# Attention and FFN in one kernel: engines in written order, value copies on ScalarE, later attention dealt out over the FFN halves

## Chip, cores and metric

One core of a Trainium2 chip. The metric is device time in microseconds (us) of one execution; the kernel before takes 285.56 us (median of three, 284.75 to 286.89). In this text PE is TensorE, PEld its weight loads, DVE is VectorE, ACT is ScalarE and POOL is GpSimd.

## The reference, cut to what matters

```python
# q, k, v: (4, 8, 768, 64); sort_net: (4, 8, 8, 8); x for the FFN: 3072 tokens x 512
P = sort_net
for _ in range(5):                       # Sinkhorn: exp, rows, columns
    P = exp(P - max(P)); P = P / P.sum(-1); P = P / P.sum(-2)
k_sorted = einsum('bhij,bhjcd->bhicd', P, k_blocks)     # 8 blocks of 96 tokens
v_sorted = einsum('bhij,bhjcd->bhicd', P, v_blocks)
attn = softmax(q_block @ k_sorted_block.T / 8)          # inside each block
x = (attn @ v_sorted_block) -> (3072, 512)
out = (silu(x @ w_gate) * (x @ w_val)) @ w_out          # d_ff = 1536
```

## The kernel before

The work falls into batches (4), each batch into two halves of 384 tokens. The K/Q step mixes blocks on PE and drains PSUM to SBUF. For V, the block index and head sit on the partitions and `(c, d)` on the free axis, so a copy first turns `(c, d)` into `(d, c)` (tile `vch`). A "unit" is QK, exp, AV, normalise, transpose for four blocks of two heads; four units give one half its input. The FFN of one half is called an FFN half below; there are eight.

```python
for it in range(N_ITER):                          # Sinkhorn, small tiles
    nc.scalar.activation(p_sb, p_sb, AF.Exp)
    nc.vector.reduce_sum(rowred[:, :, 0], p_sb, axis=AX.X)
    ...                                           # reciprocal, mul, and the same by columns

def drain(dst, src):                              # PSUM drains: DVE and ACT in turn
    if tog[0] % 2 == 0: nc.vector.tensor_copy(dst, src)
    else:               nc.scalar.copy(dst, src)
    tog[0] += 1

def emit_vch(pair):                               # pair 0 on DVE, pair 1 on GpSimd
    nat = v_tiles[pair]
    for s in range(4):
        cs = slice(s * (C // 4), (s + 1) * (C // 4))
        eng = nc.gpsimd if pair else nc.vector
        eng.tensor_copy(vch[:, :, cs], nat[:, cs, :].transpose([0, 2, 1]))
...
emit_att(0)
for b in range(B):                                # a scheduler orders the engines by priority
    if b + 1 < B: emit_att(b + 1)
    emit_gv(b, 0); emit_gv(b, 1)                  # gate and value products of both halves
    emit_out(b, 0); emit_out(b, 1)                # output products
```

The softmax here doesn't subtract the row's maximum and nothing guards it: scores larger than these inputs give would overflow.

## Time and profile before

| | before |
|---|---|
| median | 285.56 us |
| PE busy | 90% |
| first matmul, first complete FFN input, last matmul | 13.6, about 46, 281.3 us |

The page of the profile of the kernel before: busy time per engine, then rows of 40 equal slices of the span (about 7.1 us each), a digit being the busy share in tenths; PEclk is the granted PE clock.

```profile
span 285.9 us, 6221 instructions
...
PE 257.2 (90%) x2600; PEld 152.7 (53%) x2608; DVE 178.9 (63%) x383; ACT 121.7 (43%) x246; POOL 39.1 (14%) x51
...
PE   0077799969999999999999999999999999999993
...
ACT  2036745437633215976534215764332134343211
...
PEclk9999955979999999999999999999999999999999
```

PE is at 9 tenths from the sixth slice on, but for the ninth (57 to 64 us) and the last. Most of what is lost is lost before about 66 us. The chain of work that ended last, kernel before (start us, length us, what), shows how:

```profile
16.65 1.51 DVE vch L204
...
19.35 1.19 DVE vch L204
...
21.97 1.40 DVE vch L204
...
46.31 1.28 PE v_ps L297 x4
...
50.22 0.65 PE g_ps L288 x4
```

DVE copies values between the drains of K/Q, on the chain. At 46.31 us four matmuls of 384 columns take 1.28 us; at 50.22 us they take 0.65 us. That is the half clock and the full one, read from durations.

### The profile page before, as it was taken

Reading aid. Unit: us, or ns where it says so; the run is one execution under the profiler, and the core shown is the slowest. Engines: PE = TensorE matmul, PEld = TensorE weight load, DVE = VectorE, ACT = ScalarE, POOL = GpSimd, SP = SyncE. Lnnn points to the kernel's source line nnn. Section 1 sums busy time; section 2 is a strip of 40 time slices with the busy share of each in tenths; the row PEclk is TensorE's granted clock in tenths of the full one; section 3 lists DMA queues with packets and bytes.
Section 4 is the critical chain, followed back from the end, with each engine's and each line's share of the span. In section 5 each row is a group of like instructions: output and inputs, shape, how many; then the busy total and the mean of one; then the engine's idle time right before and its main releaser. Section 6 shows DMA issues by size and latency. Waiting matters only on the chain.

```text
span 285.9 us, 6221 instructions
## 1 busy us (share of the span) xinstructions
PE 257.2 (90%) x2600; PEld 152.7 (53%) x2608; DVE 178.9 (63%) x383; ACT 121.7 (43%) x246; POOL 39.1 (14%) x51
## 2 busy tenths in 40 slices
PE   0077799969999999999999999999999999999993
PEld 0066555746655446666655446666555445555441
DVE  6798746937988205789988304699885018888300
ACT  2036745437633215976534215764332134343211
POOL 8557421029500000000000000000000000000000
PEclk9999955979999999999999999999999999999999
DMA  6999999999100122000000122000000220000021
GB/s 99 198 203 197 200 213 204 220 214 214 38 0 1 39 110 76 2 2 0 3 0 2 38 110 76 2 2 2 0 0 2 111 102 10 0 0 3 37 110 73
DMA packets 13659, 20.84 MB, mean 73 GB/s; under 512 B 1088, under 2 KB 8768, under 8 KB 13632
## 3 DMA queue, kind: packets, MB, share of 16 engines
q0 software_dynamic: 10128, 14.16, 28.2%
q1 hardware_dynamic: 3504, 6.30, 5.8%
q8 instruction: 20, 0.33, 0.4%
q14 instruction: 7, 0.06, 0.1%
HBM read 28.32 MB, written 6.29 MB: 121 GB/s over the span
## 4 chain that ended last, share of the span: by engine, by line
PE 82%; DVE 11%; ACT 3%; issue 2%; ACTq 0%
PE v_ps L297 22%; PE g_ps L288 22%; PE o_ps L308 22%; PE av_ps L245 4%; PE qk L230 4%; PE tkq L193 3%; PE x_ps L255 3%; PE tv L214 3%; DVE kqt L180 2%; DVE vch L204 1%; DVE st L251 1%; ACT vt L182 1%; DVE vt L180 1%; ACT th_sb L291 1%; DVE colred L136 0%
## 5 line engine op out<-in xcount | busy, mean ns | idle before, releaser
L288 PE MATMUL g_ps<-xt,wg_sb 128*128 128x384 bf16 x384 | 84.8, 331 | 0.2 <-DVE h L299 0.2
L297 PE MATMUL v_ps<-xt,wv_sb 128*128 128x384 bf16 x384 | 82.1, 331 | 0.0
L291 ACT ACTIVATE th_sb<-g_ps 128x384 bf16<-128x384 f32 x96 | 47.1, 491 | 63.2 <-PE g_ps L288 62.6
L293 DVE SCALAR_TENSOR_TENSOR gs_sb<-th_sb,g_ps 128x384 bf16<-128x384 bf16 x96 | 52.9, 551 | 26.9 <-ACT th_sb L291 20.9
L308 PE MATMUL o_ps<-wo_sb,h 128*128 128x512 bf16 x280 | 62.4, 379 | 0.4
L299 DVE SCALAR_TENSOR_TENSOR h<-v_ps,gs_sb 128x384 bf16<-128x384 f32 x96 | 53.1, 553 | 9.0 <-PE v_ps L297 0.8
L297 PEld LDWEIGHTS <-wv_sb 128*128 128x128 bf16 x384 | 36.8, 98 | 24.5 <-issue 0.8
L288 PEld LDWEIGHTS <-wg_sb 128*128 128x128 bf16 x384 | 36.2, 99 | 23.5 <-issue 2.3
L308 PEld LDWEIGHTS <-h 128*128 128x128 bf16 x288 | 28.2, 98 | 33.6
L180 DVE CAST kqt<-tkq 128x512 bf16<-128x512 f32 x24 | 15.9, 688 | 33.9 <-PE tkq L193 33.9
L311 ACT COPY o_sb<-o_ps 128x512 f32<-128x512 f32 x24 | 14.1, 586 | 51.4 <-PE o_ps L308 51.4
L235 ACT ACTIVATE er<-qk 96x384 bf16<-96x384 f32 x64 | 27.1, 487 | 12.2 <-PE qk L230 12.2
L193 PE MATMUL tkq<-rmix,kq 128*64 128x64 bf16 x768 | 20.3, 212 | 5.5 <-issue 2.5
L193 PEld LDWEIGHTS <-kq 128*64 128x64 bf16 x768 | 17.7, 126 | 8.9 <-issue 7.9
L251 DVE TENSOR_TENSOR st<-av_ps,r_sb 96x512 bf16<-96x512 f32 x32 | 21.9, 684 | 0.8
L182 ACT CAST kqt<-tkq 128x512 bf16<-128x512 f32 x24 | 14.1, 586 | 15.7 <-PE tkq L193 15.6
L230 PE MATMUL qk<-kqt 64*128 64x96 bf16 x256 | 14.0, 217 | 1.9 <-DVE kqt L180 1.4
L245 PE MATMUL av_ps<-vt,er 96*128 96x65 bf16 x256 | 14.9, 202 | 0.2 <-ACT vt L182 0.2
L180 DVE CAST vt<-tv 96x512 bf16<-96x512 f32 x16 | 12.2, 785 | 2.7 <-PE tv L214 2.5
L182 ACT CAST vt<-tv 96x512 bf16<-96x512 f32 x16 | 12.5, 787 | 2.1 <-PE tv L214 1.8
L214 PE MATMUL tv<-vmix,vch 128*128 128x128 bf16 x128 | 12.4, 236 | 1.0 <-DVE vt L180 0.3
L255 PEld LDWEIGHTS <-st 96*128 96x128 bf16 x128 | 7.6, 101 | 10.5 <-DVE st L251 9.1
(43 smaller groups left out, 123.0 us busy)
## 6 DMA issues: line engine op xcount, KB each, us to landing
out_dram<-o_sb SPq DMA_DIRECT2D x24, 256.0 KB, 2.0
v<-in_v_dram POOLq DMA_DIRECT2D x8, 384.0 KB, 13.1
kq<-in_k_dram POOLq DMA_DIRECT2D x6, 384.0 KB, 11.6
kq<-in_q_dram POOLq DMA_DIRECT2D x6, 384.0 KB, 12.1
wg_sb<-in_moe_w_gate_dram POOLq DMA_DIRECT2D x6, 256.0 KB, 11.8
wv_sb<-in_moe_w_val_dram POOLq DMA_DIRECT2D x6, 256.0 KB, 11.1
wo_sb<-in_moe_w_out_dram POOLq DMA_DIRECT2D x1, 1536.0 KB, 18.9
kq<-in_k_dram POOLq DMA_DIRECT2D x4, 192.0 KB, 5.6
```

Of the source, the lines that this page charges most:

```text
L180: nc.vector.tensor_copy(dst, src)
L182: nc.scalar.copy(dst, src)
L193: nc.tensor.matmul(tp[two * D:(two + 1) * D, lc, :], lhsT=nat[:, cb * 8 + lc, :], rhs=rm[:, two, :], start=True, stop=True)
L230: nc.tensor.matmul(pss[two][:, i4, :], lhsT=flat[lo:lo + D, at:at + 128], rhs=kqt[lo:lo + D, 1, g, i, :], start=True, stop=True)
L235: nc.scalar.activation(e[:, 0:4 * C], pss[two][0:C].rearrange("p a c -> p (a c)"), AF.Exp, scale=scale)
L245: nc.tensor.matmul(av[:, two, i4, :], lhsT=es[two][:, i4 * C:i4 * C + 128], rhs=vt[:, 2 * g + two, half * 4 + i4, :], start=True, stop=True)
L288: nc.tensor.matmul(g_ps, lhsT=wg_sb[:, kc, ts(m, 128)], rhs=xt[:, kc, :], start=(kc == 0), stop=(kc == NKC - 1))
L291: nc.scalar.activation(th_sb, g_ps, AF.Tanh, scale=0.5)
L293: nc.vector.scalar_tensor_tensor(gs_sb, th_sb, 1.0, g_ps, op0=ALU.add, op1=ALU.mult)
L297: nc.tensor.matmul(v_ps, lhsT=wv_sb[:, kc, ts(m, 128)], rhs=xt[:, kc, :], start=(kc == 0), stop=(kc == NKC - 1))
L299: nc.vector.scalar_tensor_tensor(h_w[:, m, :], v_ps, 0.5, gs_sb, op0=ALU.mult, op1=ALU.mult)
L308: nc.tensor.matmul(o_ps, lhsT=h_w[:, m, ts(t3, 128)], rhs=wo_sb[:, m, :], start=(m == 0), stop=(m == NFC - 1))
```

## The change

The intent: fix the order of all engines until the first FFN step, take the value copies off DVE's critical place, start the FFN after four units, and deal the later attention out over the FFN halves so that PE has no attention-only stage.

```diff
+    man = tc.manual_schedule(engines={ET.PE, ET.Pool, ET.DVE, ET.Activation})
+    load_v(0, ...); load_q(0, ...); load_k(0, ...)       # then weights, then batch 1
     for it in range(N_ITER):
         nc.scalar.activation(p_sb, p_sb, AF.Exp)
+        if it >= 2:
+            copy_v(nc.scalar, 0, lowr, it - 2)           # 64 x 1536, (c d) -> (d c), on ACT
         ...
+    copy_v(nc.scalar, 0, lowr, 3)
...
+    for db in range(8):  v_chunk(0, db, "sv"[db % 2], tags[db % 2])   # batch 0 only
+    for cb in range(12): kq_chunk(0, cb, "sv"[cb % 2], tags[cb % 2])
+    for u in range(4):   ...                              # four units, then the FFN
+    man = tc.manual_schedule(engines={ET.PE, ET.Pool})    # from here only PE and POOL fixed
+    def copies(pair, rows, count):
+        return [(0.0, lambda s=s: copy_v(nc.scalar, pair, rows, s, count)) for s in range(count)]
+    merge(ffn(0), units(0, range(4, 8)) + mingle(kqs(1), copies(0, highr, 8)))
+    merge(ffn(1), [... v_chunk(1, db, "s", "att") ...] + units(1, range(4)))
+    merge(ffn(2), mingle(units(1, range(4, 8)) + kqs(2), copies(1, slice(0, 128), 8)))
+    ...                                                   # and so on to ffn(7)
-    emit_att(0)
-    for b in range(B): ...
```

In the FFN part all drains of K/Q and V are on ACT ("s"). `merge` weights pieces by an expected PE time and deals the second list out among the first.

## The prediction

> # Prediction
>
> **What bounds the kernel now.** TensorE. The page has PE 90% busy, and the chain of waits is 82% PE. Priced with dense stretches of the trace (one gate/value step 1.33 us, one output tile 2.55 us, one 8-row K/Q chunk about 0.35 us, a QK/AV/transpose unit about 0.74 us, value mixing 7 to 8 us in all), the program holds about 237 us of PE work at full clock. The last matmul ends at 281.3 us, so some 44 us are lost: 13.6 us before the first matmul (Sinkhorn), about 13 us from there to 36 us, about 12 us from 36 to 66 us, and only 6 to 7 us in the whole rest.
>
> The early losses, by the timeline: DVE does four value copies of 1.5 us between the K/Q drains (16.6 to 25.4 us); 16 value drains of 0.79 us make PE wait until 33.7 us; then units follow at 2.5 us each in a chain transpose, QK, AV, reciprocal, normalise (0.7 us). The first FFN input is complete only at about 46 us. The clock row shows half clock from about 36 to 49 us and again at 60 to 63 us, after a 2.5 us PE gap. The Trainium skill (TensorE: Matmul & The Clock Gate, Part 1) says that the clock is released only by sustained activity; the trace agrees: 384-column matmuls are 0.32 us apart until 48.9 us, then 0.16.
>
> **What changes.** Value copies for batch 0 leave DVE for ACT, between the Sinkhorn exps (estimate 1.45 us each in gaps of 1.5 us, so nearly free). Only batch 0's half of the values (8 chunks) is mixed before attention, and the FFN starts after 4 units instead of waiting behind other work. Later attention is spread over FFN halves in fixed PE order, its drains all on ACT. No PE work goes; about 1 us is added (pair 0 mixed in two halves). Loads: values first, then Q/K of batch 0, then weights; at the 200 GB/s of the page all needed for the first FFN step are there by 30 us.
>
> **On the critical path.** Matmuls start at about 13 us as before. Value chunks until 17 to 18, K/Q chunks until 23 to 25, four units at about 1.5 us each: FFN starts at 31 to 34 us, dense. Cold clock there costs about 3 us instead of about 9. Against that, fixed order brings new stalls: two AV steps back to back share one PSUM buffer (about 1 us each, four places); ACT (0.59 us K/Q drain, 0.79 us value drain, 0.49 us tanh, copies) is about as loaded as PE in the first FFN half and in the one that mixes pair 1 (2 to 3 us each). I expect 8 to 12 us of steady loss, not 6 to 7. Sum: 237 + 1 + 13 + 10 + 3 + 9 + 4.6 (tail after the last matmul) = 278; I lean a little lower, to 276.5 us.
>
> Range 268 to 285 us. Chances: faster by over 2% 0.62, within 2% 0.34, slower 0.04.
>
> **What would show it.** Right: no DVE value copies, the first FFN matmul at 31 to 34 us, clock back to full by about 40 us; PE busy about 93%; ACT busy up from 122 to about 155 us; unchanged matmul durations. Wrong: Sinkhorn ending after 12.5 us; PE waiting for ACT drains by over 8 us in total; clock low past 45 us.
>
> **What would make it wrong.** Slower: batch 1's loads land late while PE, in fixed order, waits. Faster: clock warm already during K/Q chunks, stalls hidden by PSUM buffers.

## More of the kernel before

The groups of instructions of the kernel before, by shape (out<-in, shapes, count | busy us, mean ns of one | idle before):

```profile
L182 ACT CAST kqt<-tkq 128x512 bf16<-128x512 f32 x24 | 14.1, 586 | 15.7 <-PE tkq L193 15.6
...
L204 POOL COPY vch<-v 128x1536 bf16<-128x1536 bf16 x4 | 11.2, 2878 | 0.0
...
L204 DVE COPY vch<-v 128x1536 bf16<-128x1536 bf16 x4 | 6.0, 1490 | 0.0
```

The transposing copy is on DVE and POOL here; ACT never does it. ACT's PSUM drain of 512 elements takes 586 ns. No line shows what the copy costs on ACT.

## The result, and the profile after

The changed kernel takes 298.4 us (median of four, 297.25 to 299.41), where before took 285.91 us in the runs beside it. The ratio is 1.0437 (95% interval 1.038 to 1.0494). Ratios are the mean time of one kernel's fast runs over that of the other's of the same rounds, so not quite the ratio of the medians quoted.

The page of the profile after, the same rows:

```profile
span 295.5 us, 6302 instructions
...
PE 254.5 (86%) x2672; PEld 148.6 (50%) x2672; DVE 154.2 (52%) x351; ACT 163.1 (55%) x281; POOL 18.6 (6%) x34
...
PE   0065786769999599899989899999999999999994
...
ACT  4974347996589935455787445454543353333311
...
PEclk9998559998999999999999999999999999999998
```

ACT is at 9 tenths in five of the first 14 slices (in before only in one slice, the seventeenth), and PE is at 7 tenths or less in four of those five (the second, eighth, ninth and fourteenth). The groups after, by shape, name what ACT does there:

```profile
L111 ACT COPY vch<-v 128x768 bf16<-128x768 bf16 x8 | 12.0, 1540 | 0.0
L111 ACT COPY vch<-v 64x768 bf16<-64x768 bf16 x8 | 11.9, 1506 | 0.1
...
L111 ACT COPY vch<-v 64x1536 bf16<-64x1536 bf16 x4 | 11.0, 2776 | 0.0
```

A copy of 1536 elements takes 2.78 us, not the 1.45 of the prediction; one of 768 takes 1.5 us, where the same rate would give about 0.8. Together 34.9 us of ACT, where that rate gives about 18.6 (4 x 1.45 + 16 x 0.8). The chain that ended last, after, shows that this lies on the critical path:

```profile
6.10 2.79 ACT vch L111
9.04 2.68 ACT vch L111
11.87 5.37 ACT vch L111 x2
17.29 3.59 PE tv L232 x64
...
37.93 1.28 PE v_ps L316 x4
...
53.05 0.76 PE g_ps L307 x4
...
87.74 1.40 ACT vch L111
89.14 0.76 ACT e_all L264 x2
90.16 1.53 ACT vch L111
91.69 0.77 ACT e_all L264 x2
```

From 6.1 to 17.2 us ACT copies nearly without a break; the exps of Sinkhorn stand in its queue behind copies, and the value mixing (tv) waits for the last copy. Around 90 us the copies are between the softmax exps on the chain. These are the copies of the second pair, which the code writes into the third FFN half. ACT's order is not fixed there, and the scheduler put them early: they run from 85.8 to 102.2 us, inside the second half, which ends at 108.6.

By stage, the changed kernel (window, length, PE, PEld, DVE, ACT, POOL busy, clock, DMA share, GB/s): start, first two FFN halves, the other six with the tail.

```profile
0.00:37.40 37.40, 15.80 (x355) 13.11 (x356) 21.11 (x75) 23.25 (x29) 16.52 (x30) 0.87 1.15 189
37.40:108.60 71.20, 59.68 (x643) 33.83 (x643) 34.05 (x72) 52.82 (x78) 2.06 (x4) 0.92 0.54 109
108.60:295.50 186.90, 179.04 (x1676) 101.69 (x1674) 99.07 (x204) 87.05 (x174) 0.00 (x0) 1.00 0.09 32
```

Priced as in the prediction, the first two halves hold about 52 us of dense PE work and the rest with the tail about 180 us. So 19 us are lost in the first two halves, where the prediction's sum has 9 us of steady loss for all eight and 3 for the cold clock, and only about 6 in the 187 us after. The dealt-out attention of the later halves works; the loss is early.

### The profile page after: what moved, and what is told of

Same layout as the page of the kernel before. It is cut to its first block, busy times and chain, and to the rows that moved or that the text cites. A ratio compares the mean times of both kernels' runs of the same rounds, so it can differ in the third digit from the quotient of the medians.

```text
span 295.5 us, 6302 instructions
## 1 busy us (share of the span) xinstructions
PE 254.5 (86%) x2672; PEld 148.6 (50%) x2672; DVE 154.2 (52%) x351; ACT 163.1 (55%) x281; POOL 18.6 (6%) x34
## 4 chain that ended last, share of the span: by engine, by line
PE 76%; ACT 14%; DVE 5%; issue 3%; DMA 2%; ACTq 0%; POOLq 0%
PE o_ps L326 21%; PE g_ps L307 20%; PE v_ps L316 20%; ACT vch L111 8%; PE tkq L220 5%; PE av_ps L277 3%; PE qk L257 3%; DVE st L283 2%; PE tv L232 2%; DMA v<-in_v_dram 2%; PE x_ps L294 2%; ACT e_all L264 1%; ACT th_sb L310 1%; ACT vt L189 1%; DVE gs_sb L312 1%
## 5 line engine op out<-in xcount | busy, mean ns | idle before, releaser
L307 PE MATMUL g_ps<-xt,wg_sb 128*128 128x384 bf16 x384 | 81.0, 333 | 2.5 <-ACT o_sb L329 2.2
L326 PE MATMUL o_ps<-wo_sb,h 128*128 128x512 bf16 x288 | 65.7, 379 | 0.0
L307 PEld LDWEIGHTS <-wg_sb 128*128 128x128 bf16 x384 | 32.9, 99 | 21.4 <-issue 3.0
L264 ACT ACTIVATE e_all<-qk 96x384 bf16<-96x384 f32 x64 | 27.8, 486 | 13.3 <-PE qk L257 13.1
L111 ACT COPY vch<-v 64x768 bf16<-64x768 bf16 (+2 forms) x20 | 34.9, 1774 | 0.2
L189 ACT CAST kqt<-tkq 128x512 bf16<-128x512 f32 x42 | 23.3, 591 | 11.4 <-PE tkq L220 11.3
L189 ACT CAST vt<-tv 96x512 bf16<-96x512 f32 x28 | 19.3, 746 | 4.1 <-PE tv L232 3.3
L277 PE MATMUL av_ps<-vt,e_all 96*128 96x65 bf16 x256 | 14.5, 202 | 6.6 <-DVE st L283 6.5
L277 PEld LDWEIGHTS <-e_all 96*128 96x128 bf16 x256 | 12.1, 103 | 12.3 <-DVE st L283 4.1
L281 DVE RECIPROCAL r_sb<-av_ps 96x8 f32<-96x8 f32 x32 | 6.4, 201 | 22.5 <-PE av_ps L277 22.5
## 6 DMA issues: line engine op xcount, KB each, us to landing
wg_sb<-in_moe_w_gate_dram POOLq DMA_DIRECT2D x6, 256.0 KB, 11.9
```

Source lines behind the costliest of these rows:

```text
L111: eng.copy(dst, src)
L264: nc.scalar.activation(e[:, 0:4 * C], pss[two][0:C].rearrange("p a c -> p (a c)"), AF.Exp, scale=scale)
L277: nc.tensor.matmul(o[:, two, i4, :], lhsT=e[:, i4 * C:i4 * C + 128], rhs=vt[:, 2 * g + two, half * 4 + i4, :], start=True, stop=True)
L307: nc.tensor.matmul(g_ps, lhsT=wg_sb[:, kc, ts(m, 128)], rhs=xt[:, kc, :], start=(kc == 0), stop=(kc == NKC - 1))
L326: nc.tensor.matmul(o_ps, lhsT=h_w[:, m, ts(t3, 128)], rhs=wo_sb[:, m, :], start=(m == 0), stop=(m == NFC - 1))
```

## Experiments

Ten kernels ran, in three calls; those of one call (e1 to e4; e5 to e8; e9 and e10) shared a chip and the runs of the kernel before. e1 and the runs that build on it thus ran on different chips. Told by the ratios, the gains on e1 are 4.3 (e5), 5.2 (e6), 5.3 (e7) and 2.3 us (e8), so within 0.3 us of the differences of medians given below. Theory A: ACT, made slow by the copies, holds up both the start and the first FFN halves. Rival B: the fixed order itself (one PSUM buffer for AV, the half clock). Theory C: it is the strided access that makes the copies slow on ACT; rival D: ACT is that slow for any such copy.

| run | what | median us | ratio to before (95%) |
|---|---|---|---|
| changed kernel | | 298.40 | 1.0437 (1.038 to 1.0494) |
| e1 | FFN copies on POOL | 287.53 | 1.0055 (0.9996 to 1.0113) |
| e2 | FFN copies on DVE | 290.25 | 1.0169 (1.0107 to 1.0232) |
| e3 | copies read in order, write strided | 359.33 | 1.2581 (1.2523 to 1.2639) |
| e4 | half of the start copies on POOL | 298.21 (fast ones alone 297.61) | 1.0433 (1.0371 to 1.0495) |
| e5 | e1, start copies split finer | 282.88 | 0.9904 (0.9866 to 0.9941) |
| e6 | e1, PE kept busy until the FFN | 282.32 | 0.9874 (0.9844 to 0.9904) |
| e7 | e1, no start copies (wrong result) | 282.43 | 0.9869 (0.9825 to 0.9913) |
| e8 | e1, AV steps spread | 285.46 | 0.9973 (0.9932 to 1.0015) |
| e9 | e1, e5, e6 and e8 together | 279.07 | 0.9758 (0.9725 to 0.979) |
| e10 | changed kernel, plain copies (wrong result) | 283.34 | 0.9906 (0.986 to 0.9953) |

### e1: the FFN part's copies on POOL

```diff
-        return [(0.0, lambda s=s: copy_v(nc.scalar, pair, rows, s, count)) for s in range(count)]
+        return [(0.0, lambda s=s: copy_v(nc.gpsimd, pair, rows, s, count)) for s in range(count)]
```

Expected: 

> All else as in the changed kernel; only the 16 value copies of the FFN part (23.8 us of ACT work at about 1.5 us each in the trace, against 0.8 us that the prediction assumed) go from ACT to GpSimd. Theory A (ACT, overloaded by these copies in the first two FFN halves, holds PE up): those two halves lose about 19 us against dense work, some 4 of it to the half clock; 12 to 15 us come back, so 283 to 287 us, and ACT is no longer 100% busy anywhere between 85 and 100 us. Rival B (the fixed PE order itself, with the one PSUM buffer of AV and the half clock): at most 4 us come back, 294 us or more.

Measured: 287.53 us, 10.9 us less. PE's order did not change by one instruction. The stages of e1, for the two stages after the start:

```profile
37.90:98.70 60.80, 57.81 (x639) 33.52 (x642) 34.17 (x72) 30.61 (x62) 26.44 (x22) 1.00 0.62 127
98.70:286.00 187.30, 178.16 (x1660) 101.69 (x1674) 99.07 (x204) 87.05 (x174) 0.00 (x0) 1.00 0.09 32
```

ACT's busy time in the first two halves falls from 52.8 to 30.6 us and the stage from 71.2 to 60.8; the rest stays at 187. A copy is no shorter on POOL (1.50 and 1.52 us) than on ACT; but POOL has nothing else to do there. The gain is a little under the range expected (it was 12 to 15), but it is A's, and B's limit of 4 us is passed.

### e2: the same copies on DVE

```diff
+        return [(0.0, lambda s=s: copy_v(nc.vector, pair, rows, s, count)) for s in range(count)]
```

Expected: 

> The same 16 copies on DVE, which is 52% busy. Theory A: about as e1, 283 to 288 us; a DVE copy of 64x768 should take about 0.8 us (half of the 1.49 us that 128x1536 took on DVE before), so DVE has room. Rival B: 294 us or more. If e1 gains and e2 does not, then not ACT's load but the place of the copies matters.

Measured: 290.25 us. The copies take 0.82 us each on DVE, as expected, and most of the gain is there: it is 2.7 us smaller than with POOL. In the trace PE waits 2.0 us for DVE's gate step where e1 has none: the copies stand in DVE's queue before it. The expected range missed that by about 2 us.

### e3: read in memory order, write strided (edit condensed)

```diff
-        dst = vch3[rows, :, cs];                  src = v_tiles[pair][rows, cs, :].transpose([0, 2, 1])
+        dst = vch3[rows, :, cs].transpose([0, 2, 1]);  src = v_tiles[pair][rows, cs, :]
```

Expected: 

> All value copies stay on ACT; each reads the values in memory order and writes transposed, where the changed kernel reads with a 128-byte stride and writes runs. Theory C (the strided SBUF read of 2-byte elements is what makes ACT take 1.8 ns per element where its PSUM drains take 0.84): a 64x1536 copy falls from 2.78 to about 1.5 us, a 768 one from 1.5 to 0.8 us, FFN starts 3 to 4 us earlier, and the whole takes 279 to 285 us. Rival D (any SBUF to SBUF 16-bit copy on ACT, or the strided write, costs as much): durations and time stay as they are, 296 to 300 us.

Measured: 359.33 us. Neither outcome came; the groups of e3:

```profile
L113 ACT COPY vch<-v 128x768 bf16<-128x768 bf16 x8 | 31.8, 4124 | 0.0
L113 ACT COPY vch<-v 64x768 bf16<-64x768 bf16 x8 | 31.8, 4114 | 0.1
L113 ACT COPY vch<-v 64x1536 bf16<-64x1536 bf16 x4 | 31.1, 8054 | 0.0
```

Writing with the stride is far worse than reading with it: 8.05 us for 1536 elements against 2.78. So the access pattern matters greatly, and the strided read was the better of the two. This does not yet say what a copy without any stride costs; e10 does.

### e4: two of the four start copies on POOL

```diff
+    copy_v(nc.gpsimd, 0, lowr, 1); copy_v(nc.gpsimd, 0, lowr, 3)      # before the weight loads
-        if it >= 2:
+        if it in (2, 4):
             copy_v(nc.scalar, 0, lowr, it - 2)
```

Expected: 

> Only the start: two of the four Sinkhorn-time copies move to GpSimd (ahead of its weight loads), the others stay on ACT after the exps 3 and 5. Theory A for the start (11 us of ACT copies from 6.1 to 17.2 us set when value mixing can begin): value matmuls start at about 15 us instead of 17.3, and the FFN about 2 us earlier; 295 to 297 us in all. Against it: if weight loads, now issued after the copies, come late, PE waits for weights and the time grows over 299 us.

Measured: 298.21 us, no gain (one of the four executions, 302.33 us, was slow; the median of the others is 297.61); value matmuls began at 16.95 us instead of 17.29. The timeline of e4 (start, length, engine, line, operation) shows why:

```profile
6.19 5.74 POOL L113 COPY vch<-v 64x1536 bf16<-64x1536 bf16 x2 [1.20 <-DMA v<-in_v_dram]
...
6.64 2.68 DVE L175 TENSOR_TENSOR p_sb<-p_sb,rowred 32x64 f32<-32x64 f32 x1
...
9.87 2.14 DVE L179 TENSOR_TENSOR p_sb<-p_sb,colred 32x64 f32<-32x64 f32 x1
```

The small multiply of Sinkhorn, 0.21 us elsewhere, takes 2.68 and 2.14 us while POOL copies: the POOL copies end at 9.24 and 11.93 us, and each multiply ends 0.08 us later. The Trainium skill (GPSIMD Engine Reference, section 8, Key points) says that POOL shares its SBUF interfaces with VectorE and contends with DVE instructions that have two SBUF inputs. This multiply is such an instruction, and the trace agrees. DVE's sums and reciprocals between them keep their 0.2 us. ACT's delay of the Sinkhorn chain was traded for one on DVE. In the FFN part DVE's gate step and product read PSUM as one operand; in e1 they take 553 and 555 ns on average as in the changed kernel, so no such hold shows.

### e5: start copies in eighths, over ACT and DVE

```diff
-            copy_v(nc.scalar, 0, lowr, it - 2)            # 64 x 1536
+            copy_v(nc.scalar, 0, lowr, it - 2, 8)         # 64 x 768, fits the gap
-    copy_v(nc.scalar, 0, lowr, 3)
+    for s in (3, 4):    copy_v(nc.scalar, 0, lowr, s, 8)
+    for s in (5, 6, 7): copy_v(nc.vector, 0, lowr, s, 8)
```

Expected: 

> Against e1 (copies of the FFN part on GpSimd, 287.5 us), only the start differs: the Sinkhorn-time copies are eight pieces of 64x768 (1.48 us on ACT, which fits the 1.5 us between two exps), one after each of the exps 3 to 5, two more on ACT and three on DVE (0.8 us each) after Sinkhorn. Theory (in e1 each 2.77 us copy holds the next exp up by about 1.3 us and the last ends at 17.2 us): value mixing starts at about 15.4 us instead of 17.3, FFN 2 us earlier; 285 to 286 us. Rival (what follows is bound by loads or by the half clock): no gain, 287 us.

Measured: 282.88 us, 4.6 us less than e1, more than expected. The timeline of e5, ACT:

```profile
6.18 1.50 ACT L111 COPY vch<-v 64x768 bf16<-64x768 bf16 x1
...
7.67 0.26 ACT L163 ACTIVATE p_sb<-p_sb 32x64 f32<-32x64 f32 x1
7.83 1.47 ACT L111 COPY vch<-v 64x768 bf16<-64x768 bf16 x1
...
9.43 0.26 ACT L163 ACTIVATE p_sb<-p_sb 32x64 f32<-32x64 f32 x1
```

Now the exps come about 1.8 us apart, so the short copies fit, and value mixing starts at 14.39 instead of 17.31 us. Of the 4.6 us the trace shows 3.2 as the earlier start: the last matmul of the first gate step begins at 34.70 instead of 37.91 us. The rest was not foreseen: the clock is full again at 41.0 us in e5's trace, at 49.7 in e1's, so one gate/value step fewer runs at half clock (about 1.3 us).

### e7: no copies of batch 0 at the start (wrong result)

```diff
-            copy_v(nc.scalar, 0, lowr, it - 2)
-    copy_v(nc.scalar, 0, lowr, 3)
+            nc.tensor.matmul(tp[:, ld, :], lhsT=vch[rows, at:at + 128] if b else fake[rows], rhs=mix,
```

Expected: 

> Wrong result on purpose: e1 without any copy of batch 0's values; the value mixing of batch 0 reads a constant tile instead. It bounds what the start's copies cost. Theory: exps run 1.76 us apart, last Sinkhorn step done by 11.7 us, value mixing at 13.5 to 14 us instead of 17.3; total 283.5 to 284.5 us if the 3.4 us come through whole. If less than 1.5 us come through, K/Q loads or the clock take over.

Measured: 282.43 us; value mixing starts at 12.48 us. The start's copies cost 5.1 us in e1. e5, with a right result, gets 4.6 us, but by the start alone it gets 3.2 of 5.4: the first gate step's last matmul begins at 32.54 us here.

### e6: PE kept busy until the FFN

```diff
+    def keep_warm(n):
+        w = psum.tile([128, TW], FP32, name="warm_ps", tag="gen")
+        for _ in range(n):
+            nc.tensor.matmul(w, lhsT=ident, rhs=warm, start=True, stop=True)   # never read
```

Expected: 

> e1 with 26 idle-filling matmuls on PE (128x384, results unused): 8 before the value mixing, 4 before the first QK, 2 per unit, 6 before the FFN. Theory (half clock: in e1 the 384-column matmuls are 0.32 us apart until about 49 us, 0.16 after 53; four gate/value steps and the four units pay 4 to 6 us for it): matmuls at 0.16 us spacing from before 40 us and 282 to 285 us. Rival (the waits for DVE and ACT in the units are what counts, and the fillers only stand in the way): 287 to 289 us.

Measured: 282.32 us, 5.2 us less than e1. The chain of e1, then that of e6 (start, length, what):

```profile
46.27 1.28 PE g_ps L307 x4
...
53.47 0.65 PE g_ps L307 x4
```

```profile
36.24 0.65 PE g_ps L309 x4
36.89 0.65 PE v_ps L318 x4
```

In e1 the gate step still takes 1.28 us at 46 us; in e6 it takes 0.65 us from the first. The half clock is thus worth about 5 us in e1, where the prediction had 3. The clock comes back late in e1: the clock record is at full from 49.7 us there, and from 44.7 us in the changed kernel, so it may cost less there. In e1's profile the clock row says 1.00 throughout, against its own matmul durations; the record has no entry before 49.7 us, and here the durations are to be believed.

### e8: AV steps spread

```diff
-                todo.append((0.27, lambda u=us[n - 1]: av(b, u)))
+                todo.append((0.6, lambda u=us[n - 1]: av(b, u)))
```

Expected: 

> e1 with AV steps weighted 0.6 instead of 0.27 when side work is dealt out, so that in nearly all places a gate/value step stands between two AV steps, which share one PSUM buffer. PE waited 6.5 us in e1 for the normalisation before an AV, about 2.3 of it in the start where nothing changes. Theory: 2 to 4 us gained, 283.5 to 285.5 us. Rival (other waits appear at the same places, as two QK steps now stand together at the start of a half): within 1 us of e1.

Measured: 285.46 us, 2.1 us under e1, in the expected range, but the two intervals overlap (0.9932 to 1.0015, 0.9996 to 1.0113). PE's wait for the normalisation before an AV falls from 6.5 to 1.2 us (waits of e1, then of e8: total us, times, longest):

```profile
PE av_ps L277 <- DVE st L283: 6.5, 8, 1.4
```

```profile
PE x_ps L294 <- DVE st L283: 2.9, 3, 1.3
...
PE av_ps L277 <- DVE st L283: 1.2, 3, 0.6
```

But 2.9 us of waits for it now stand before the transposes (0.4 in e1) and 3.5 us of waits for ACT before QK (1.1 in e1). So most of the wait moved, as the rival said. The clock was also full 3.0 us earlier than in e1 (46.7 against 49.7 us). How much of the 2 us is the spreading is not shown.

### e10: plain copies (wrong result)

```diff
-        dst = vch3[rows, :, cs]
-        src = v_tiles[pair][rows, cs, :].transpose([0, 2, 1])
+        run = slice(s * (C // n) * D, (s + 1) * (C // n) * D)
+        dst = vch[rows, run]
+        src = v_tiles[pair][rows].rearrange("p c d -> p (c d)")[:, run]
```

Expected: 

> Wrong result on purpose: the changed kernel with nothing moved; every value copy on ACT copies as many elements of the same type between the same tiles, but read and written in memory order, without the transpose. Theory C: such a copy takes what the prediction assumed, 0.8 us for 768 and 1.45 us for 1536 elements (0.84 ns per element), exps are no longer held up, and the kernel takes 283 to 287 us; the wrong duration is then worth 11 to 15 of the 22 us between prediction and result, and half clock and the AV waits are the rest. Rival D: ACT needs 1.7 ns per element for any copy between SBUF tiles of 16-bit elements; the durations stay 1.5 and 2.8 us and the time 297 to 300 us.

Measured: 283.34 us. The groups of e10:

```profile
L112 ACT COPY vch<-v 128x768 bf16<-128x768 bf16 x8 | 6.6, 844 | 0.0
...
L112 ACT COPY vch<-v 64x768 bf16<-64x768 bf16 x8 | 6.4, 827 | 0.1
...
L112 ACT COPY vch<-v 64x1536 bf16<-64x1536 bf16 x4 | 5.8, 1460 | 0.1
```

These are the durations that the prediction's rate gives (0.8 and 1.45 us) nearly to the digit, on the same engine and tiles. So rival D falls: an ACT copy between SBUF tiles is not slow as such. Theory C holds in this, that the transposing access is what made it slow; that the strided side must be the read was refuted by e3. Per element, by the difference of the two lengths: (1460 - 827) / 768 = 0.82 ns plain, (2776 - 1506) / 768 = 1.65 ns with the transposing read, (8054 - 4114) / 768 = 5.1 ns with the transposing write. The chain of e10:

```profile
12.54 3.57 PE tv L233 x64
...
32.94 0.48 PE g_ps L308
```

Value mixing starts at 12.54 us, as early as with no copies at all (12.48 in e7): at the assumed duration the copies do fit the gaps and are "nearly free". The last matmul of the first gate step begins at 32.94 us, inside the predicted 31 to 34.

### e9: the fixes together

The edit is those of e1, e5, e6 and e8 together.

Expected: 

> e5, e6 and e8 together on e1 (which ran 287.5 us): start copies split over ACT and DVE, PE kept busy up to the FFN, AV steps spread, FFN copies on GpSimd. They gained 4.6, 5.2 and 2.0 us one at a time. If they are separate losses, 275 to 278 us and a ratio to the kernel before of 0.963 to 0.972, faster than both kernels. If they overlap (the clock's gain is had already by the earlier start, or the instruction stall at 22 to 25 us eats it), 279 to 282 us.

Measured: 279.07 us, ratio 0.9758 (0.9725 to 0.979): 2.4% faster than the kernel before and 6.5% faster than the changed one (279.07 / 298.4). One by one the three steps on e1 gained 4.6 + 5.2 + 2.1 = 11.9 us; together 8.5. So they overlap, as the second outcome said. The page of e9:

```profile
span 277.3 us, 6355 instructions
...
PE 249.0 (90%) x2698; PEld 146.0 (53%) x2698; DVE 155.0 (56%) x354; ACT 135.3 (49%) x266; POOL 43.1 (16%) x51
```

Part of the overlap is visible. e5 alone has already shortened the half clock, which e6 cannot win again. And a wait of PE in the K/Q chunks that the page puts down to "issue" grows from 1.6 us in e1 to 3.1 us in e9. PE gets there earlier, and the wait ends less early (22.3 us in e9, 25.3 in e6, 26.4 in the changed kernel). In all eleven traces of the new order it begins after the same 222 matmuls, whatever their mix, and even in e3, where that point comes at 44.9 us. The packed traces list the packets of each DMA queue: in all eleven PE goes on 1.4 to 1.6 us after a 16 KB packet of the queue called "instruction" has ended. The 2.5 us wait at 57.4 us in the kernel before, at whose end the clock fell to half for the second time, also ends 1.5 us after such a packet. So PE most likely waits there for its next instructions (the "instruction stall" of the expectation); no run moved the fetch to test it.

## Why the prediction was wrong, point by point

- **Where the time lay before: right.** The last six halves run in 187 us in the changed kernel and in e1, about 6 us over the priced PE work. The dealt-out attention costs nearly nothing there.
- **The step that failed: "estimate 1.45 us each in gaps of 1.5 us, so nearly free".** A 64x1536 copy took 2.78 us and overran the gaps; the 768 ones took 1.5 instead of 0.8 us. No trace had this copy on ACT; the rate is that of ACT's PSUM drains (e3's expectation puts them at 0.84 ns per element). The copy reads SBUF elements of 2 bytes 128 bytes apart. The Trainium skill (SBUF — State Buffer, "Door 1: The DMA port swizzle") has a note that warns of such access: consecutive accesses in the same 16-byte line go at full speed, and each crossing to a new line pays. It names no engine and gives no size. The runs agree that the stride costs (1.65 against 0.82 ns per element on ACT); none varied the distance, so that the 16-byte line is the reason is not shown. The prediction did not use the note.
- **What that one duration was worth: 15.1 us** of the 21.9 us between forecast and result (298.4 to 283.3 in e10). Both of its places show: the start (e7: 5.1 us of copies in e1) and the first two halves (e1: 10.9 us). They add to 16, about the 15.1, so they look nearly separate; but e7 and e1 take copies off ACT altogether, where e10 makes them short. The second place was also not the planned one: the prediction looked for an overloaded ACT in the first half and in the one that mixes pair 1 (the fourth). The copies of pair 1 are written into the third, and ACT ran them in the second.
- **FFN start at 31 to 34 us, Sinkhorn by 12.5 us: wrong, for the same reason.** Sinkhorn's last step ended at 13.9 us. The first gate step was complete only at about 37.9 us, and in e10 at 33.4. One lone matmul of that step did run at 33.84 us, between the units, so the literal sign "first FFN matmul at 31 to 34 us" came true by luck; the dense FFN that it stood for came late.
- **Cold clock "about 3 us": too small as far as shown.** Keeping PE busy gained 5.2 us on e1 (e6), whose half clock lasted until 49.7 us. In the changed kernel half clock lasted until 44.7 us, not 40.
- **AV stalls, about 4 us: right in kind,** 6.5 us of waits in the changed kernel's and e1's traces. e8 moved most of them elsewhere, and its gain of about 2 us isn't clear of noise.
- **ACT load: right in kind, wrong in size.** Foreseen 155 us, measured 163.1; the copies are 16 us over, the drains somewhat under. "2 to 3 us" of ACT-bound loss in the first half became a large share of 19 us over two halves.
- **The sign.** The chance given to slower by over 2% was 0.04. The whole forecast gain was 9 us, and one duration never seen in the trace, used 20 times on an engine planned full, was worth more.

What stays open: of the 6.8 us between e10 and the forecast, the clock (about 2 us over what was allowed, if e6's gain on e1 carries over) and ACT's remaining load in the first halves (63.2 us from 32.9 to 96.1 us in e10, against 60.8 in e1) are measured in part; 1.5 us was a lean without a reason. The rest was not separated. The moment at which the clock is full again differs between the traces (41.0 us in e5, 49.7 in e1), so a difference of 1 to 2 us between two of these runs can be the clock's alone.

## What to carry to other kernels

Before an operation is moved to another engine, look for a duration of that same access pattern on that engine; if the trace has none, the estimate is a guess and the range must hold twice its size. A copy that has to sit inside a latency chain must be cut to fit the gap, or it moves the chain itself (in e5 value mixing starts 2.9 us earlier, by halving the pieces and sharing them). When PE runs in written order, one late engine stops it, so plan the fullest side engine with slack in each stage, not on average; and where that engine's own order is left to a scheduler, look in the trace for the stage in which its work really ran.

## What the Trainium skill lacked or had wrong

- SBUF — State Buffer, "Door 1: The DMA port swizzle": no size for crossing 16-byte lines on ACT. The runs: 0.82 ns per 2-byte element in order, 1.65 ns reading with a 128-byte stride, 5.1 ns writing with a 192-byte stride. On DVE the same strided read of 768 elements took 0.82 us, on POOL 1.5 us.
- ScalarE: Activation LUTs, "What ACT_TABLE_LOAD costs": one element per cycle, 0.833 ns, for every function. That holds for the plain copy (0.82 ns in e10) and not for the transposing one; the page does not say so.
- Runtime: NRT & Kernel Launch, "Instruction fetch mechanics": says that crossing a block of 256 instructions is mostly hidden. In eleven traces PE stood for 1.2 to 3.3 us after the same 222 matmuls and went on 1.4 to 1.6 us after a 16 KB packet of the instruction queue had ended. If that is the fetch, which fits but was not tested, it is not hidden there.
